# Three fillers in the second and third burst, and fixed steps for the lots between bursts

## The chip, the cores and the metric

One Trainium2 chip, one of its cores. The metric is the device time of one execution of the kernel in microseconds; lower is better.

## The reference

```python
def sm(a, b):                                  # softmax of scaled scores
    s = (a @ b.transpose(0, 2, 1)) / np.sqrt(128)
    e = np.exp(s - s.max(-1, keepdims=True))
    return e / (e.sum(-1, keepdims=True) + 1e-09)
agent_v = sm(agents, k) @ v                    # 4 batches, 49 agents, 12480 keys, width 128
x = (sm(q, agents) @ agent_v).reshape(49920, 128)
h = x @ w_in                                   # 128 x 2048
out = (h * np.cos(h)) @ w_out                  # 2048 x 128
```

All arrays are fp32 (the two weight arrays are float64 on input). Each batch first needs a softmax of 49 agents over its 12480 keys and the product with the values; then each token needs a softmax over 49 agents and a feed-forward layer with h * cos(h).

## The kernel before, in words

Tokens are worked in groups of 960; a batch has 13 groups, the four batches 52. After a start-up of some 65 us, which deals with the keys and values of the first batch, one loop runs over 832 **steps**, 16 for a group. A step does three things: `first_product(n)` (L853, two TensorE matmuls into one of three `ph` tiles in PSUM, then a Sin on ScalarE into `c`, L856), `cubic_part` (L862, one VectorE instruction that makes `r` from `c` and `ph`, and by that frees the `ph` tile), and `second_product(n - 4)` (L878, two matmuls that add into a small PSUM tile `one`; every eighth step ScalarE copies the sum out, L880).

All other work is slipped into these steps by a hand-written plan. Its pieces, called **lots** here, are for the batch that comes next or for groups that come later:

- a **query** (`query_parts`, L510): 16 short matmuls into a small tile `one` (L152), a copy of it to `e` (L527; by VectorE in a burst, by ScalarE elsewhere), the row maximum (L531, VectorE), a subtraction on GpSimd (L533);
- a **values** lot (`add_values`, L585): an addition to `es` on GpSimd (L286), 16 matmuls into a small tile `one` (L301), and their sum taken by VectorE (L307 the first time, L309 later);
- **scores** of the next batch's keys (13 for a batch), and for each group `query_weights` and `query_turned` (L591, L600 to L608), whose steps are the same in both kernels.

Only two small tiles `one` exist (`ps_1`, bufs=2), and one of them is held by the running sum of `second_product`. So one is left for the lots: each must wait until VectorE or ScalarE has emptied the tile of the lot before it.

Exp and Sin are in different ScalarE tables. The Exps are therefore gathered in **bursts**: at step 109, 133 and 157 of each block of 208 steps (`BURSTS`, a block makes one next batch, so there are three blocks with such bursts) ScalarE loads the table of Exp, does one Exp for four or five queries (L575, `query_exp`) and one for four or five groups of keys (L279, `pinned_exp`), and loads the table of Sin again. During that no Sin runs, so no `r` is made and no `ph` tile comes free; `fill(at, todo)` puts up to three lots into this stretch. The first goes into step `at`, the second into step `at + 1` between the sums of the first two queries (L578, VectorE, which wait for the Exp) and the sums of the rest, the third is split over steps `at + 2` and `at + 3`. In the six steps from a burst the order of TensorE, VectorE and ScalarE is held as written.

What `fill` does not take goes into later steps by `extra(n, ...)`, which takes the first free step from n on at certain places of the period of eight (three of eight, or five of eight with `dense=True`).

Of the kernel before, what the change touches and what calls it, by code (L numbers as in the profile page):

```python
# [42 lines left out]
def agent_attention_cos_ffn(ctx, tc, qT, kT, v, v0, v0_rest, agT, w_in, w_out, outT):  # L43
# [432 lines left out]
    with ExitStack() as pools:  # L476
# [145 lines left out]
        BURSTS = (109, 133, 157)  # L622
# [80 lines left out]
        def extra(n, f, *args, dense=False):  # L703


            while n in taken or (n - LAG) % NP not in ((1, 2, 3, 4, 5) if dense else (1, 3, 5)):
                n += 1
            taken.add(n)
            plan(n, f, *args)
            return n  # L710
# [5 lines left out]
        def spread_out(todo, t, end):  # L716

            for i, lot in enumerate(todo):
                t = extra(t, *lot) + 1
                if i + 1 < len(todo):  # L720
                    t += max(0, (end - t) // (len(todo) - i - 1) - 1)
            return t
# [14 lines left out]
        def burst(t, piece, keys=None):  # L737
            assert t + 4 < piece[0] * STEP - 10
            windows.add(t)
            plan(t, query_exp, piece)  # L740
            if keys:
                plan(t, pinned_exp, *keys)
            sums.extend((n, t) for n in piece)
            plan(t + 5, query_inverse, piece)

        def scored(piece, *how):
            return [(query, n, piece, *how) for n in piece]

        def fill(at, todo):

            taken.update(range(at, at + 3))
            parts = [in_parts(*todo.pop(0)) for _ in range(min(3, len(todo)))]
            if parts:
                plan(at, list, parts[0])
            early_plan(at + 1, summed, at, 2)
            if len(parts) > 1:
                early_plan(at + 1, list, parts[1])
            early_plan(at + 1, summed, at, 9)
            for x, n in zip(parts[2:], range(at + 2, at + 9)):
                early_plan(n, next, x)  # L760
                (early_plan if n + 1 < at + 5 else plan)(n + 1, list, x)

        t = spread_out(scored(early), 0, 0) + 2
# [5 lines left out]
        for b in range(1, NB):  # L769
            o, ps = (b - 1) * PER, pieces[b - 1]  # L770

            def valued(k):
                return [(add_values, ab[b], g) for g in range(lots[k][0], sum(lots[k]))]

            qs, ks = scored(ps[0])[ahead:], [(ab[b].scores, g) for g in range(3 if b == 1 else 0, NG)]
            both = []
            while qs or ks:
                both += ks[:3] + qs[:1]
                ks, qs = ks[3:], qs[1:]
            t = spread_out(both, t, o + BURSTS[0] - 14)  # L780
            plan(t, ab[b].top)
            t = extra(t, ab[b].across)
            t = extra(t + 1, ab[b].spread)
            assert t < o + BURSTS[0], (t, o)
            for g, n in lots:
                plan(t, ab[b].shift, g, n, nc.gpsimd)
            nxt = scored(pieces[b][0], False, True)[:2]
            ahead = len(nxt)
            fresh = [scored(ps[1], False, True), scored(ps[2], False, True), nxt]
            for k, at in enumerate(BURSTS):  # L790
                at += o
                burst(at, ps[k], (ab[b], *lots[k]))
                vs, qs = valued(k - 1) if k else [], fresh[k]
                todo = []
                for x in ("qqqqqqq", "vq", "vq")[k]:
                    z = vs if x == "v" else qs
                    if z:
                        todo.append(z.pop(0))
                fill(at, todo)
                t = at + 6  # L800
                if k == 2:
                    vs += valued(2)
                qs, todo = todo, []
                qs += [x for x in fresh[k] if x not in qs]
                qs = [x[:3] if x[0] is query else x for x in qs]
                while vs or qs:
                    todo += qs[:1] + vs[:1]
                    vs, qs = vs[1:], qs[1:]
                if k == 0:
                    todo += [x[:3] for x in fresh[1][:2]]  # L810
                    del fresh[1][:2]
                end = o + BURSTS[min(k + 1, 2)] - 4
                for i, x in enumerate(todo):
                    t = extra(t, *x, dense=k == 2) + (2 if k == 2 else 1)
                    assert k == 2 or x[0] is not query or t < o + BURSTS[k + 1], (t, o, k)
                    if k < 2 and i + 1 < len(todo):
                        t += max(0, (end - t) // (len(todo) - i - 1) - 1)
            plan(t, ab[b].total)
            t = extra(t, ab[b].folded) + 1
            t = extra(t, ab[b].inverse) + 1  # L820
            i = b % 2
            for c in range(DFF // 512):
                t = extra(t, ab[b].project, c, a[i], dense=True) + 1
            t = extra(t, ab[b].project_out, wio, b1[i], b2[i], dense=True)
            plan(t, ab[b].judge)
            t += 1
            assert t < o + PER + 2, (t, o + PER)
        at = (NB - 1) * PER + BURSTS[0]
        t = spread_out([x for piece in pieces[NB - 1] for x in scored(piece)][ahead:], t, at - 6)
# [231 lines left out]
```

## Time and profile before

| | |
|---|---|
| median of 3 runs | 1180.17 us (1177.71 to 1183.73) |
| the profiled execution: its own time | 1180.92 us |
| its span, first to last instruction | 1179.1 us |
| TensorE, VectorE, ScalarE, GpSimd busy | 95%, 90%, 83%, 30% |
| mean granted TensorE clock | 0.977 |

Busy shares are averages over stages with different limits, and a TensorE that runs at half its clock counts as busy. Granted clock 1.00 is 2.4 GHz; the other level is half of it.

### The profile page before, as it was taken

How to read it: one execution, taken by the hardware profiler on the slowest of the kernel's cores; microseconds unless marked ns; L12 is line 12 of the kernel's file. 1: busy time of each engine (PE TensorE's matmuls, PEld its weight loads, DVE VectorE, ACT ScalarE, POOL GpSimd, SP SyncE). 2: the span in 40 equal slices, each digit the busy share in tenths (PEclk: the TensorE clock that was granted, in tenths of full speed). 3: DMA queues.
4: the chain of work that ended last, by engine and by line, in shares of the span. 5: the costliest groups of instructions: out<-in, count | busy, mean ns of one | idle time of the engine just before them, and what ended most of it. 6: DMA issues, size and time to landing. Idle time of an engine off the chain costs nothing.

```text
span 1179.1 us, 17151 instructions
## 1 busy us (share of the span) xinstructions
PE 1122.9 (95%) x6239; PEld 901.8 (76%) x6239; DVE 1061.0 (90%) x1205; ACT 980.1 (83%) x1234; POOL 349.9 (30%) x389
## 2 busy tenths in 40 slices
PE   6899999999999999999899999998999999989996
PEld 3677888787778888787777888877777777767774
DVE  5779999997899999998789999998878999999996
ACT  4778888898678888888778888898777899998995
POOL 1032131752313131463323122264331223122320
PEclk9999999998999999999899999999989999999998
DMA  9733324523201223263220322354240000000001
GB/s 362 288 93 108 101 84 135 167 85 106 96 34 54 91 74 95 81 181 114 85 84 17 101 67 84 106 152 130 68 118 34 34 34 18 34 17 34 18 34 37
DMA packets 37520, 107.74 MB, mean 91 GB/s; under 512 B 4162, under 2 KB 4770, under 8 KB 37426
## 3 DMA queue, kind: packets, MB, share of 16 engines
q1 hardware_dynamic: 37426, 106.55, 28.0%
q8 instruction: 52, 0.85, 0.3%
q14 instruction: 42, 0.34, 0.1%
HBM read 80.97 MB, written 25.56 MB: 90 GB/s over the span
## 4 chain that ended last, share of the span: by engine, by line
PE 70%; DVE 15%; ACT 9%; issue 4%; DMA 1%; SPq 0%; POOL 0%; ACTq 0%; DVEq 0%
PE ph L853 26%; PE one L878 22%; DVE r L862 12%; PE one L152 10%; ACT c L856 5%; PE one L301 3%; PE one L874 2%; PE one L600 2%; PE one L875 1%; DMA c<-qT 1%; PE ph L451 1%; PE one L346 1%; ACT osb L880 1%; ACT L575 1%; ACT s L279 1%
## 5 line engine op out<-in xcount | busy, mean ns | idle before, releaser
L862 DVE SCALAR_TENSOR_TENSOR r<-c,ph 128x960 fp32r<-128x960 f32 x832 | 916.1, 1148 | 60.3 <-ACT c L856 49.7
L856 ACT ACTIVATE c<-ph 128x960 f32<-128x960 f32 x832 | 785.3, 980 | 110.9 <-PE ph L853 99.3
L853 PE MATMUL ph<-pT,a 113*128 113x480 f32 x1664 | 540.2, 404 | 19.7 <-DVE r L862 18.4
L878 PE MATMUL one<-r,w 128*128 128x480 f32 x1664 | 505.4, 392 | 2.1 <-ACT osb L880 1.7
L853 PEld LDWEIGHTS ph<-pT,a 113*128 113x128 f32 x1664 | 293.8, 191 | 134.9 <-DVE r L862 73.6
L878 PEld LDWEIGHTS one<-r,w 128*128 128x128 f32 x1664 | 312.3, 192 | 54.9 <-issue 4.8
L152 PEld LDWEIGHTS one<-ag,xt 128*120 128x120 f32 x1408 | 164.3, 188 | 14.1 <-DVE sums L307 4.2
L152 PE MATMUL one<-ag,xt 128*120 128x49 f32 x1408 | 160.9, 268 | 5.5 <-DVE sums L307 3.0
L591 POOL TENSOR_TENSOR p<-e,rz 120x392 f32<-120x392 f32 x51 | 42.9, 846 | 323.7 <-PE one L600 252.2
L608 POOL TENSOR_TENSOR pT<-p,pT 49x480 fp32r<-49x480 f32 x102 | 124.2, 1217 | 7.8
L533 POOL TENSOR_TENSOR e<-e,mx 120x392 f32<-120x392 f32 x49 | 41.4, 844 | 225.9 <-DVE mx L531 225.6
L607 POOL CAST pT<-p 49x480 fp32r<-49x480 f32 x102 | 59.4, 583 | 114.7 <-ACT p L604 110.1
L880 ACT COPY osb<-one 128x480 f32<-128x480 f32 x104 | 57.9, 557 | 4.1 <-PE one L878 4.1
L301 PE MATMUL one<-vt,s 120*49 120x128 f32 (+1 forms) x624 | 44.9, 289 | 5.2 <-DVE sums L309 5.2
L301 PEld LDWEIGHTS one<-vt,s 120*49 120x49 f32 (+1 forms) x624 | 35.1, 136 | 17.9 <-issue 8.1
L286 POOL TENSOR_TENSOR es<-es,s 120x392 f32<-120x392 f32 x36 | 36.8, 1023 | 37.2 <-ACT s L279 35.5
L275 POOL TENSOR_TENSOR s<-s,mxb 120x1568 f32<-120x1568 f32 (+1 forms) x9 | 31.5, 3534 | 34.1 <-DVE mxb L271 34.1
L875 PE MATMUL one<-pT,b 113*128 113x480 f32 x104 | 39.9, 384 | 0.0
L874 PE MATMUL one<-pT,b 113*128 113x480 f32 x104 | 39.9, 384 | 0.0
L248 ACT COPY s<-one 120x392 f32<-120x392 f32 x36 | 17.5, 487 | 20.8 <-PE one L152 20.8
L527 ACT COPY e<-one 120x392 f32<-120x392 f32 x34 | 16.6, 487 | 20.3 <-PE one L152 20.3
L600 PEld LDWEIGHTS one<-ident,p 120*113 120x113 f32 x204 | 28.6, 179 | 4.6 <-ACT a L347 0.9
(143 smaller groups left out, 542.7 us busy)
## 6 DMA issues: line engine op xcount, KB each, us to landing
outT<-osb SPq DMA_DIRECT2D x51, 480.0 KB, 2.6
xt<-qT SPq DMA_DIRECT2D x49, 480.0 KB, 3.6
xt<-kT SPq DMA_DIRECT2D x39, 480.0 KB, 3.5
vt<-v SPq DMA_DIRECT2D x78, 240.0 KB, 3.9
xt<-kT SPq DMA_DIRECT2D x7, 512.0 KB, 7.7
vt<-v SPq DMA_DIRECT2D x6, 512.0 KB, 5.2
c<-kT SPq DMA_DIRECT2D x5, 512.0 KB, 6.9
vt<-w_in SPq DMA_DIRECT2D x8, 256.0 KB, 7.2
```

The costliest lines, as they stand in the source:

```text
L152: mm = nc.tensor.matmul(ps[:, t, :], xt[:, t * TT:(t + 1) * TT], ag[:, b, :], start=True, stop=True)
L301: mm = nc.tensor.matmul(po[h * HI:h * HI + width], e[:, x * NA:x * NA + width], vt[:, x, :], start=(t == 0), stop=(t == HT - 1))
L600: mm = nc.tensor.transpose(pt[:KR, t * TT:(t + 1) * TT], p_in[n % 2][:, t, :KR], ident[:TT, :TT])
L607: nc.gpsimd.tensor_copy(pT[own, c], p[own])
L608: nc.gpsimd.tensor_sub(pT[other, c], p[own], pT[own, c].bitcast(F32))
L853: nc.tensor.matmul(ph[:, j, :CH], ai[:, f], pTs[q % 3][:, c], start=True, stop=True)
L856: nc.scalar.activation(cos, h, AF.Sin, bias=HALF_PI, scale=1.0)
L862: nc.vector.scalar_tensor_tensor(r, cos, 1.0, h, op0=ALU.subtract, op1=ALU.mult)
L874: nc.tensor.matmul(po, b1[k], pTs[q % 3][:, c], start=False, stop=False)
L875: nc.tensor.matmul(po, b2[k], pTs[q % 3][:, c], start=False, stop=False)
L878: nc.tensor.matmul(po, w1[:, f, :], r[:, j, :], start=(f == 0), stop=(f == NF - 1))
L880: nc.scalar.copy(osb[:, c * CH:(c + 1) * CH], po)
```

## The change

The kinds of the lots that `fill` gets are changed from up to seven queries, "values, query", "values, query" for the three bursts of a block to "query, query, query" and twice "query, values, query". (In the first burst there are three queries either way, as `fill` takes at most three.) The lots after the first burst get steps 117, 125 and 129 of the block, those after the second 141, 145, 149 and 151, in place of an even spread; the lots after the third follow each other as before.

By the rules of `extra` and `fill` the steps of the lots come out so (steps within a block; "b" is in the burst):

| stretch | before | after |
|---|---|---|
| first burst | query b109, b110, b111 | the same |
| up to the second | query 117, 125, 129 | the same |
| second burst | values b133, query b134 | query b133, values b134, query b135 |
| up to the third | query 141, values 143, query 149, values 151 | query 141, values 145, 149, 151 |
| third burst | values 157 (ahead of the Exps), values b157, query b158 | query b157, values b158, query b159 |
| after it | query 165, values 167, 173, 175, 177, 181, 183, 189, 191 | values 165, 167, 173, 175, 177, 181, 183, 189 |
| end of the block | folded 193, inverse 197, project 198, 199, 200, 205, project_out 206 | 191, 193, 197, 198, 199, 200, 205 |

```diff
@@ -792,7 +792,7 @@
                 burst(at, ps[k], (ab[b], *lots[k]))
                 vs, qs = valued(k - 1) if k else [], fresh[k]
                 todo = []
-                for x in ("qqqqqqq", "vq", "vq")[k]:
+                for x in ("qqq", "qvq", "qvq")[k]:
                     z = vs if x == "v" else qs
                     if z:
                         todo.append(z.pop(0))
@@ -809,12 +809,12 @@
                 if k == 0:
                     todo += [x[:3] for x in fresh[1][:2]]
                     del fresh[1][:2]
-                end = o + BURSTS[min(k + 1, 2)] - 4
+                steps = (((117, 125, 129), (141, 145, 149, 151))[k] if k < 2 else ())
                 for i, x in enumerate(todo):
-                    t = extra(t, *x, dense=k == 2) + (2 if k == 2 else 1)
-                    assert k == 2 or x[0] is not query or t < o + BURSTS[k + 1], (t, o, k)
-                    if k < 2 and i + 1 < len(todo):
-                        t += max(0, (end - t) // (len(todo) - i - 1) - 1)
+                    if i < len(steps):
+                        assert t <= o + steps[i], (t, steps)
+                        t = o + steps[i]
+                    t = extra(t, *x, dense=True) + (2 if k == 2 else 1)
             plan(t, ab[b].total)
             t = extra(t, ab[b].folded) + 1
             t = extra(t, ab[b].inverse) + 1
```

## Rows read from the trace of the kernel before

**Rows 1.** The page: engines' busy time, and the granted clock in forty slices.

```profile
PE 1122.9 (95%) x6239; PEld 901.8 (76%) x6239; DVE 1061.0 (90%) x1205; ACT 980.1 (83%) x1234; POOL 349.9 (30%) x389
...
PEclk9999999998999999999899999999989999999998
```

**Rows 2.** Windows (start:end, length, busy by engine, PEclk), cut at starts of Sins.

```profile
214.03:228.74 14.71, 13.81 (x83) 11.32 (x84) 13.53 (x19) 13.51 (x14) 14.26 (x12) 1.00 0.76 209
...
249.63:263.71 14.08, 12.59 (x70) 10.26 (x70) 12.05 (x16) 13.63 (x15) 7.63 (x9) 0.88 0.35 106
263.71:285.69 21.98, 21.51 (x137) 17.87 (x136) 19.88 (x23) 17.34 (x22) 5.66 (x8) 1.00 0.30 90
285.69:304.36 18.67, 16.52 (x83) 13.69 (x84) 12.75 (x20) 14.17 (x14) 7.86 (x8) 0.73 0.27 80
304.36:339.53 35.17, 34.85 (x245) 28.18 (x245) 31.29 (x35) 26.50 (x33) 9.61 (x11) 1.00 0.26 85
...
568.22:586.71 18.49, 15.05 (x83) 12.13 (x84) 13.02 (x20) 14.08 (x14) 7.85 (x8) 0.82 0.28 80
...
814.69:830.36 15.67, 12.62 (x70) 10.26 (x70) 12.18 (x16) 13.72 (x15) 8.68 (x10) 0.89 0.30 94
...
1093.99:1111.57 17.58, 17.17 (x73) 12.41 (x73) 17.24 (x17) 16.18 (x20) 4.46 (x6) 1.00 0.08 29
...
1120.15:1148.44 28.29, 27.72 (x119) 20.25 (x118) 27.63 (x27) 26.28 (x32) 7.21 (x8) 1.00 0.09 36
```

**Rows 3.** Groups of ScalarE instructions in the first block's third burst.

```profile
L856 ACT ACTIVATE c<-ph 128x960 f32<-128x960 f32 x8 | 7.7, 984 | 4.5 <-PE ph L853 4.4
L575 ACT ACTIVATE e<-e 120x1960 f32<-120x1960 f32 x1 | 1.8, 1837 | 0.0
```

**Rows 4.** Timeline of TensorE, first block's third burst (start, us, engine line [idle before]).

```profile
286.42 1.09 PE L301 MATMUL one<-vt,s 120*64 120x128 f32 x16
289.22 1.97 PE L301 MATMUL one<-vt,s 120*64 120x128 f32 x16 [1.72 <-DVE sums L309]
...
292.89 3.28 PE L152 MATMUL one<-ag,xt 128*120 128x49 f32 x16
```

**Rows 5.** Timeline of TensorE, first block's first burst.

```profile
217.84 1.88 PE L152 MATMUL one<-ag,xt 128*120 128x49 f32 x16 [0.47 <-DVE e L527]
219.54 0.69 PE L878 MATMUL one<-r,w 128*128 128x480 f32 x2
220.07 0.60 PE L853 MATMUL ph<-pT,a 113*128 113x480 f32 x2
220.50 1.78 PE L152 MATMUL one<-ag,xt 128*120 128x49 f32 x16
```

**Rows 6.** Timeline of TensorE, first block's second burst.

```profile
249.98 1.09 PE L301 MATMUL one<-vt,s 120*64 120x128 f32 x16
...
253.14 2.26 PE L152 MATMUL one<-ag,xt 128*120 128x49 f32 x16 [1.00 <-DVE sums L307]
```

**Rows 7.** Groups of instructions, whole run (count, busy us, mean ns).

```profile
L531 DVE TENSOR_REDUCE mx<-e 120x8 f32<-120x392 f32 x49 | 27.2, 556 | 2.1 <-ACT e L527 0.4
...
L309 DVE TENSOR_TENSOR sums<-sums,one 113x128 f32<-113x128 f32 x36 | 10.1, 281 | 6.1 <-PE one L301 6.1
...
L527 DVE COPY e<-one 120x392 f32<-120x392 f32 x15 | 8.4, 562 | 9.8 <-PE one L152 9.7
```

**Rows 8.** Timeline of VectorE and ScalarE, the same first burst.

```profile
217.23 0.56 DVE L527 COPY e<-one 120x392 f32<-120x392 f32 x1
217.24 1.51 ACT L575 ACTIVATE e<-e 120x1568 f32<-120x1568 f32 x1
...
218.78 1.03 DVE L578 TENSOR_REDUCE rz<-e 120x8 f32<-120x392 f32 x2 [0.33 <-ACT e L575]
...
219.76 0.57 DVE L527 COPY e<-one 120x392 f32<-120x392 f32 x1
```

**Rows 9.** Transfers issued: queue, count, KB each, median us to landing.

```profile
xt<-qT SPq DMA_DIRECT2D x49, 480.0 KB, 3.6
```

## The prediction

> **What bounds the kernel now.** I read the page first: TensorE is busy for 95% of the span, VectorE for 90%, ScalarE for 83%, and the granted clock dips at a few places only [rows 1]. Shares that near to each other name no bound, so I read it by stage. I cut the steps at the starts of Sins: eight steps of a burst, the 16 or 26 steps behind it, and the same stretches in the fourth block, which has no lots but `query_turned` [rows 2]. In the first block the three bursts take 14.71, 14.08 and 18.67 us for the same eight steps. The reader is to see in those rows which engine fills the stretch. In the second burst ScalarE is busy for 13.63 of 14.08 us: two table loads, two Exps, eight Sins and two copies leave 0.45 us, so nothing that TensorE does there can shorten it much. In the third burst ScalarE is busy for 14.17 of 18.67 us and VectorE for 12.75; the clock is 0.73, so TensorE ran at its lower level for over half of the stretch. That burst is the one with slack: 4.5 us of each.
>
> What ended ScalarE's idle time there is `ph` [rows 3]: 4.4 of 4.5 us wait for `first_product`. TensorE's timeline says why [rows 4]. Two values lots stand one behind the other. The second waits 1.72 us for the small tile, until VectorE has got through the `cubic_part`s queued ahead of the sum; after that gap the clock halves, and the query behind it takes 3.28 us where a query at full clock takes 1.78 [rows 5]. Its VectorE copy, the sums and all later `r` are late by as much, and so is `ph`. The second burst has the same in small: a gap of 1.00 us behind a values lot [rows 6], clock 0.88. In the first burst, where a query comes first, the gap is 0.47 us [rows 5] and the clock stays at 1.00 [rows 2]. The other blocks repeat this: the second burst takes 14.09 us in the second block (the row of the first stands for it) and 15.67 in the third; the third takes 18.49 in the second (clock 0.82) and 18.67 in the third, as in the first.
>
> **The change part by part.** No instruction is added or removed. In each of three blocks two queries move from the steps between bursts into the bursts, and one values lot moves out of the third burst.
>
> *Lots between bursts.* The 16 steps behind the second burst hold two queries and two values lots and take 21.98 us; the same steps with neither take 17.58 in the fourth block: 4.40 us for four lots. The 26 steps behind the third hold one query and eight values lots: 35.17 against 28.29, 6.88 us for nine [rows 2]. If all four cost the same, a query is 1.10 and a values lot 1.10; if both stretches are solved together, a query is 1.52 and a values lot 0.67. I take 1.3 and 0.9. After the change two queries are gone and one values lot has come: -2 x 1.3 + 0.9 = -1.7 us a block, -5.1 in all; the ends are -3.3 (1.10 and 1.10) and -7.1 (1.52 and 0.67). Fixed steps themselves move one lot by two steps (143 to 145) and the block's end by one or two; I cost that at nothing, because the number of lots in the stretch is the same and the deadline of the next block's weights is its own first steps.
>
> *Third burst.* It gets query, values, query in place of values, values, query. VectorE has one copy (0.56) and one maximum (0.56) more and one sum (0.28) less [rows 7]: 12.75 + 0.84 = 13.6 us, still under ScalarE's 14.17. So ScalarE is the floor. What comes on top is the overhang of a burst: 14.71 - 13.53 = 1.2 us in the first burst, whose order of lots the new one resembles, 0.45 in the second [rows 2]. I take 1.0, nearer to the first: 15.2 us. The three third bursts go from 55.83 (18.67 + 18.49 + 18.67) to 45.6: -10.2. The lower end is 14.6 each (-11.9); the upper takes the overhang of the worst second burst, 15.67 - 13.72 = 1.95: 16.1 each (-7.5).
>
> *Second burst.* One query more: VectorE 12.05 + 1.12 = 13.2 us, ScalarE 13.63 as before (a burst's query is copied by VectorE). 13.63 + 1.0 = 14.6 each; three of them 43.8 against 43.84 now: 0. Ends: 14.08 each (-1.6) and 15.6 (+2.9).
>
> *The new wait.* The middle lot is now a values lot, and the third lot must wait for its sum. VectorE does that sum behind the sums of two queries, which wait for the Exp. In the first burst's times [rows 5, 8]: the middle lot starts at 217.84, would end 1.09 us later [rows 6], then come `second_product` and `first_product`, so TensorE is at the third lot at about 219.8. VectorE ends the two sums at 219.81 and the values' sum at 220.1: a gap of about 0.3 us, and some 0.6 in the third burst, whose Exp takes 1.84 [rows 3] in place of 1.51 [rows 8]. Behind the waiting lot on TensorE stand `second_product` and the next `first_product`; their Sins can't run before the table of Sin is back, so ScalarE hides a wait of this size. The gap ahead of the middle lot becomes that of the first burst, about 0.5 us; I bound it by 0.9 in the second burst, whose VectorE ends its `cubic_part`s later.
>
> *A rule that speaks against it.* The gap ends whenever VectorE empties the one free small tile, and that was so in all three bursts [rows 4, 5, 6]; but its size went with the lots' order, from 1.72 to 0.47 us. The Trainium skill, page "Perfetto Trace Analysis", section "Optimization Strategy", holds that the same gap coming back for a stretch can mean that there is too little SBUF or PSUM for the next tile. By that the change, which adds no tile, would leave the gaps, and the time would be that of the second rival below. The sum goes by the rows.
>
> *Transfers.* The moved queries need their 480 KB earlier; one lands in 3.6 us [rows 9]. Three buffers rotate: the query at step 135 takes the buffer that the one at 125 leaves, ten steps earlier, at 1.1 us or more each (17.58 / 16). The first six values lots of a block have six buffers that were left in the block before. So I cost transfers at nothing; without that cover a query would wait up to 3.6 us.
>
> Sum against the profiled execution's 1180.92 us (0.06% above the median of the runs): -10.2 + 0 - 5.1 = -15.3, so 1165.6. With the low ends together 1180.92 - 11.9 - 1.6 - 7.1 = 1160.3, with the high ones 1180.92 - 7.5 + 2.9 - 3.3 = 1173.
>
> **Rivals.** *All of the lost clock comes back.* The share of clock lost in second and third bursts is 0.27 x 18.67 twice, 0.18 x 18.49, 0.12 x 14.08 twice and 0.11 x 15.67 [rows 2]: 18.5 us. If TensorE were what sets the time in all of it, the kernel would take 1180.92 - 18.5 - 5.1 = 1157. Against it: ScalarE's busy time leaves 0.45 us in two of the second bursts, 1.95 in the other and 4.5 in a third. The Trainium skill, "TensorE: Matmul & The Clock Gate", section "Terms", prices a throttled stretch in this way, its length times the share of clock withheld. 7%.
>
> *The bursts still lose the clock.* Two gaps, 0.5 to 0.9 and 0.3 to 0.6 us, now stand close together, and a single one of 1.00 was enough in second bursts [rows 6]. If each burst drops for a short while, as the third block's second burst (15.67 against 14.08, 1.6 us more), third bursts take 16.8 (-5.4), second bursts 16.2 (+4.8), and with the moved lots (-3.3 to -5.1) it comes to 1175 to 1177, within 0.5% of now. 13%.
>
> *Slower: the third lot waits as long as the second values lot does now.* If VectorE has `cubic_part`s or sums queued so that the gap ahead of the third lot reaches 1.7 us, both bursts go as the third does today, and the third lot itself runs at half clock (3.28 for 1.78, +1.5). Third bursts 20.2 (+4.7), second ones 20.2 less the 0.6 us of their shorter Exps, 19.6 (+15.0), lots -5.1: 1195.5. It decides from a gap of about 1.7 us; I work out 0.3 to 0.6. 6%, with a little for whatever else is slower.
>
> **How the numbers follow.** 74% for the forecast; its own range is 1160 to 1173. The predicted time is its sum, 1165.6. The range of 1158 to 1176 adds half of the rival that still loses the clock and leaves out the rest. 0.5% of the time (5.9 us) is about what a measurement of this kernel can tell from no change; below 1174.3 is faster. Faster 0.80 (the forecast and the first rival, less a little of its upper end), same 0.14, slower 0.06.
>
> **What would show it.** In the profile after: third bursts of 15 to 16 us and a clock near 1.00 where 0.73 stood; second bursts about as long as now; 16 steps behind the second burst shorter by 0.4 to 1 us, 26 steps behind the third by 1.1 to 1.5; ScalarE's wait for `ph` in the third burst below 1 us; the gap ahead of the middle lot about 0.5 us and ahead of the third about 0.3 to 0.6. I am wrong if the clock dips stay, if second bursts grow by over 1 us, or if the steps behind the bursts take back what the bursts give.

## The result, and the profile after

The changed kernel takes 1165.14 us (median of 5 runs, 1164.99 to 1169.49), the kernel before beside it 1177.76 us: a ratio of 0.9881, 95% interval 0.9855 to 0.9906. The prediction was 1165.6 us, range 1158 to 1176. The profiled spans are 1179.1 and 1163.3 us, 15.8 us apart.

The windows of the changed kernel, cut at the same Sins as [rows 2]: second burst, 16 steps behind it, third burst, 26 steps behind that, the last 18 steps of the block (all of the first block), and the second burst of the third block:

```profile
250.48:265.43 14.95, 12.91 (x85) 10.20 (x85) 12.72 (x18) 13.79 (x15) 7.85 (x10) 1.00 0.54 161
265.43:286.78 21.35, 21.27 (x138) 17.06 (x136) 19.88 (x24) 16.58 (x21) 5.53 (x7) 1.00 0.29 93
286.78:302.06 15.28, 13.62 (x84) 10.45 (x84) 13.11 (x19) 14.19 (x14) 8.78 (x9) 1.00 0.14 45
302.06:336.48 34.42, 34.42 (x245) 27.16 (x245) 31.35 (x37) 25.99 (x31) 8.78 (x10) 1.00 0.30 96
336.48:359.91 23.43, 22.93 (x99) 16.61 (x97) 22.30 (x30) 20.90 (x26) 7.00 (x10) 1.00 0.05 21
806.38:821.32 14.94, 12.91 (x85) 10.19 (x85) 12.71 (x18) 13.78 (x15) 7.84 (x10) 1.00 0.51 159
```

The one of these stretches of before that [rows 2] does not hold is the end of the block, from the windows of the kernel before:

```profile
339.53:363.42 23.89, 23.66 (x112) 16.86 (x111) 22.08 (x29) 20.37 (x26) 6.33 (x9) 1.00 0.06 22
```

The reader is to see three things in these rows. The third burst fell from 18.67 to 15.28 us with the same eight Sins, and ScalarE's busy time in it did not move (14.17 and 14.19). Its granted clock is 1.00 in place of 0.73; all six changed bursts stand at 1.00. The second burst grew from 14.08 to 14.95 us, at a clock that rose from 0.88 to 1.00. And the steps between are shorter: over three blocks, third bursts went from 55.83 to 45.86 (-10.0), second bursts from 43.84 to 44.83 (+1.0), the 16 steps by -1.9, the 26 steps by -2.4, the ends of the blocks by -1.4; together -14.6 (added before rounding) of the span's 15.8. The other 1.2 us lie in steps whose lots are the same in both kernels, which differ by up to 0.9 us either way: the last block's burst took 15.04 and 14.17, and the first block's first burst began at 214.03 and 214.95.

TensorE's timeline in the first block's third burst after the change, to be read beside [rows 4]:

```profile
287.39 1.78 PE L152 MATMUL one<-ag,xt 128*120 128x49 f32 x16
...
290.59 1.09 PE L301 MATMUL one<-vt,s 120*64 120x128 f32 x16 [0.47 <-DVE e L527]
...
293.12 1.88 PE L152 MATMUL one<-ag,xt 128*120 128x49 f32 x16 [0.38 <-DVE sums L309]
...
297.07 0.70 PE L853 MATMUL ph<-pT,a 113*128 113x480 f32 x2 [0.69 <-DVE r L862]
```

The gap of 1.72 us is gone; three smaller ones stand in its place, and the query's matmuls take 1.88 us where they took 3.28. ScalarE's Sins in that burst wait 0.5 us for `ph` in place of the 4.4 of [rows 3]:

```profile
L856 ACT ACTIVATE c<-ph 128x960 f32<-128x960 f32 x8 | 7.5, 984 | 0.6 <-PE ph L853 0.5
```

The second burst after the change, from the timeline of all engines:

```profile
254.26 1.09 PE L301 MATMUL one<-vt,s 120*64 120x128 f32 x16 [0.78 <-DVE e L527]
...
256.15 0.28 DVE L307 COPY sums<-one 113x128 f32<-113x128 f32 x1
...
258.89 2.22 DVE L862 SCALAR_TENSOR_TENSOR r<-c,ph 128x960 fp32r<-128x960 f32 x2 [1.52 <-ACT c L856]
...
261.03 0.56 DVE L527 COPY e<-one 120x392 f32<-120x392 f32 x1
261.64 0.67 PE L600 MATMUL one<-ident,p 120*113 120x120 f32 x4 [0.84 <-DVE e L527]
```

Here the gap ahead of the middle lot is 0.78 us, there is none ahead of the third (its query at 256.48 has no wait in the timeline), and the third lot's tile is emptied late: its copy at 261.03 stands behind two `cubic_part`s, for the first of which VectorE sat idle for 1.52 us. The matmuls of `query_turned`, which need the tile, wait 0.84 us for it.

### The profile page after: what moved, and what is told of

The parts are those of the page before. It is cut to its first block, busy times and chain, and to the rows that moved or that the text cites. A ratio compares the mean times of both kernels' runs of the same rounds, so it can differ in the third digit from the quotient of the medians.

```text
span 1163.3 us, 17163 instructions
## 1 busy us (share of the span) xinstructions
PE 1110.6 (95%) x6239; PEld 885.4 (76%) x6239; DVE 1063.5 (91%) x1211; ACT 978.4 (84%) x1228; POOL 350.2 (30%) x389
## 4 chain that ended last, share of the span: by engine, by line
PE 65%; DVE 17%; ACT 11%; issue 5%; DMA 1%; SPq 0%; POOL 0%; ACTq 0%; DVEq 0%
PE ph L853 25%; PE one L878 20%; DVE r L862 14%; PE one L152 8%; ACT c L856 6%; PE one L301 3%; PE one L875 1%; PE one L874 1%; PE one L600 1%; DMA c<-qT 1%; ACT L575 1%; PE ph L451 1%; ACT osb L880 1%; ACT s L279 1%; PE one L346 1%
## 5 line engine op out<-in xcount | busy, mean ns | idle before, releaser
L878 PE MATMUL one<-r,w 128*128 128x480 f32 x1664 | 499.9, 388 | 1.4 <-ACT osb L880 1.1
L853 PEld LDWEIGHTS ph<-pT,a 113*128 113x128 f32 x1664 | 288.8, 189 | 135.5 <-DVE r L862 82.7
L878 PEld LDWEIGHTS one<-r,w 128*128 128x128 f32 x1664 | 307.8, 189 | 50.6 <-issue 4.3
L152 PEld LDWEIGHTS one<-ag,xt 128*120 128x120 f32 x1408 | 160.2, 185 | 13.5 <-DVE e L527 3.0
L152 PE MATMUL one<-ag,xt 128*120 128x49 f32 x1408 | 157.9, 265 | 3.8 <-DVE e L527 1.8
L608 POOL TENSOR_TENSOR pT<-p,pT 49x480 fp32r<-49x480 f32 x102 | 124.0, 1216 | 7.8
L607 POOL CAST pT<-p 49x480 fp32r<-49x480 f32 x102 | 59.4, 583 | 114.7 <-ACT p L604 109.8
L880 ACT COPY osb<-one 128x480 f32<-128x480 f32 x104 | 57.9, 557 | 4.8 <-PE one L878 4.8
L301 PEld LDWEIGHTS one<-vt,s 120*49 120x49 f32 (+1 forms) x624 | 33.0, 130 | 17.2 <-issue 9.0
L301 PE MATMUL one<-vt,s 120*49 120x128 f32 (+1 forms) x624 | 42.4, 278 | 3.8 <-DVE e L527 3.8
L275 POOL TENSOR_TENSOR s<-s,mxb 120x1568 f32<-120x1568 f32 (+1 forms) x9 | 31.5, 3530 | 34.2 <-DVE mxb L271 34.2
L600 PE MATMUL one<-ident,p 120*113 120x120 f32 x204 | 29.9, 268 | 2.5 <-DVE e L527 2.5
```

Of the source, the lines that this page charges most:

```text
L152: mm = nc.tensor.matmul(ps[:, t, :], xt[:, t * TT:(t + 1) * TT], ag[:, b, :], start=True, stop=True)
L301: mm = nc.tensor.matmul(po[h * HI:h * HI + width], e[:, x * NA:x * NA + width], vt[:, x, :], start=(t == 0), stop=(t == HT - 1))
L600: mm = nc.tensor.transpose(pt[:KR, t * TT:(t + 1) * TT], p_in[n % 2][:, t, :KR], ident[:TT, :TT])
L607: nc.gpsimd.tensor_copy(pT[own, c], p[own])
L608: nc.gpsimd.tensor_sub(pT[other, c], p[own], pT[own, c].bitcast(F32))
L853: nc.tensor.matmul(ph[:, j, :CH], ai[:, f], pTs[q % 3][:, c], start=True, stop=True)
```

## Experiments

The theory: a gap on TensorE lets its clock fall, and at the low clock `ph` comes late for ScalarE; that was most of the third burst's excess. Rivals: the clock only follows, and VectorE's queue and the place of the lots make the burst long; or what gains is the third lot under the Exps. A **dip** is here a stretch in which the granted clock is at its lower level, and the **later place** is the `first_product` behind the Exps that waits for the first `cubic_part` to free a `ph` tile. Where no interval is given, a kernel was measured in one execution. Spans are those of the profiled runs (before 1179.1, changed 1163.3). The diffs are against the changed kernel unless told otherwise.

**More work in the gap.** The kernel before, with two values lots of a block (the first of the second burst and the one at step 157) multiplied twice.

```diff
-            for t in range(HT):
+            for again in range(2 if g in (0, 3) and ordered[0] else 1):
+                for t in range(HT):
...
```

> The kernel before, with the 16 matmuls of the first values lot of the second burst and of the values lot at step 157 done twice into the same tile (the second time starts the sum anew, so the output is the same). TensorE gets about 1.1 us more work just ahead of the gap. Theory (the gap lets the clock fall, and the low clock makes the third burst long): the gap in the third burst shrinks from 1.72 to about 0.7 us and the one in the second from 1.00 to about 0, the clock stays at 1.00, third bursts take 15.5 to 16.5 us in place of 18.6, second ones 14.1 to 14.5; the span is 6 to 9 us shorter although work was added. Rival (VectorE's queue and the place of the lots make the burst long, the clock only follows): third bursts stay at 18.6 or grow by up to 1 us, the span is 0 to 3 us longer.

It measured 1172.07 us (median of 8 runs; ratio to before 0.9934, interval 0.9911 to 0.9957), span 1170.2. The third bursts and, last but one, a second burst in its windows:

```profile
286.21:301.72 15.51, 12.96 (x99) 10.72 (x100) 12.85 (x20) 13.98 (x14) 7.87 (x8) 1.00 0.34 96
565.70:581.22 15.52, 12.95 (x99) 10.71 (x100) 12.86 (x20) 13.98 (x14) 7.87 (x8) 1.00 0.34 97
809.06:824.74 15.68, 13.51 (x86) 11.13 (x86) 12.11 (x16) 13.75 (x15) 8.58 (x10) 0.89 0.29 95
846.71:862.22 15.51, 12.95 (x99) 10.71 (x100) 12.86 (x20) 13.97 (x14) 7.87 (x8) 1.00 0.44 128
```

And TensorE's timeline in the first third burst (this kernel's lines stand one lower, L302 for L301):

```profile
286.93 1.96 PE L302 MATMUL one<-vt,s 120*64 120x128 f32 x32
289.74 1.09 PE L302 MATMUL one<-vt,s 120*64 120x128 f32 x16 [0.85 <-DVE sums L310]
...
297.40 0.67 PE L854 MATMUL ph<-pT,a 113*128 113x480 f32 x2 [1.61 <-DVE r L863]
```

Work was added, no lot was moved, and the kernel became 0.66% faster. The gap is 0.85 us, the clock stays at 1.00, and each third burst is 3.0 to 3.2 us shorter, 9.3 us for the three. The second values lot starts 3.5 us into the burst in both kernels, so the wait for VectorE ahead of it ends as late as before, and the clock is what differs. This is the theory's case and rules out the first rival. In the second burst the gap behind the values lot went, but one of 2.07 us stood at the later place; the bursts took 14.11, 14.09 and 15.67, as before. A burst with two lots has a second place at which TensorE runs dry.

Where in a burst the dip falls decides what it costs. The kernel before in its first and its third second burst, each cut ahead of the dip and in it:

```profile
249.63:254.40 4.77, 3.77 (x34) 2.80 (x34) 3.33 (x5) 4.74 (x6) 0.00 (x0) 1.00 0.65 200
254.50:257.85 3.35, 3.35 (x12) 2.93 (x12) 2.94 (x6) 3.32 (x3) 1.98 (x2) 0.50 0.44 119
...
814.69:824.45 9.76, 6.71 (x49) 5.12 (x48) 7.64 (x12) 9.70 (x10) 3.52 (x4) 1.00 0.49 151
824.55:827.85 3.30, 3.30 (x11) 2.86 (x12) 2.98 (x3) 1.66 (x3) 2.70 (x5) 0.50 0.00 0
```

In the first the dip lies under the second Exp and the load of the Sin table: ScalarE is busy for 3.32 of its 3.35 us, and the burst of 14.08 us is as long as those of 14.09 and 14.11 that have no dip. In the second it comes at the later place: ScalarE is busy for 1.66 of 3.30 us, and the burst takes 15.67.

**The order alone.** Query before values in the burst; the values lot at step 157 stays.

```diff
-                for x in ("qqq", "qvq", "qvq")[k]:
+                for x in ("qqq", "qv", "qv")[k]:
-                steps = (((117, 125, 129), (141, 145, 149, 151))[k] if k < 2 else ())
+                steps = (((117, 125, 129), (141, 143, 149, 151, 157))[k] if k < 2 else ())
```

> Two lots in the second and third burst as before, but the query first and the values second; every other lot at its step of before, the values lot at step 157 ahead of the third burst too. Theory: second bursts lose their gap of 1.00 us and the dip, 14.1 to 14.3 us; in the third burst the query now waits for the sum of the values lot at 157, the gap of about 1.7 us and the low clock stay, 17.5 to 19 us; the span is within 3 us of before. Rival (query first is what counts in itself): third bursts fall to 15 to 16 us, the span by some 9 us.

Span 1178.3. Third bursts 17.8, 17.8 and 17.8; TensorE's timeline in the first shows the gap where the theory puts it, and the query behind it at half clock:

```profile
290.10 3.43 PE L152 MATMUL one<-ag,xt 128*120 128x49 f32 x16 [1.73 <-DVE sums L309]
```

The second bursts did not all get the 14.1 us I expected: 14.10, 15.68 and 15.68, all three with a gap of 2.45 to 2.47 us at the later place, and the last two with a dip there. The rival (query first is what counts) is out: the third bursts did not fall to 15 or 16 us.

**The lot at step 157 alone.** Values, query in the bursts, but no lot within six steps ahead of the third.

```diff
-                for x in ("qqq", "qvq", "qvq")[k]:
+                for x in ("qqq", "vq", "vq")[k]:
-                steps = (((117, 125, 129), (141, 145, 149, 151))[k] if k < 2 else ())
+                steps = (((117, 125, 129), (141, 143, 145, 149, 151))[k] if k < 2 else ())
```

> Bursts as before (values, query), but the values lot at step 157 goes to step 145, so that no lot stands within six steps ahead of the third burst. Theory: the third burst becomes like the second of before, a gap of about 1.0 us and at most a short dip, 14.7 to 16.5 us; the three values lots between cost about 0.9 us each; the span is 5 to 8 us shorter. Rival (the third lot under the Exps is what gains): third bursts stay above 17.5 us, the span is within 2 us of before.

Span 1175.5: 3.6 us gained where I expected 5 to 8, as two of the three third bursts, 17.08, 14.71 and 17.09 us, lie above the 14.7 to 16.5 that I gave. Its windows show those of the first and the second block, with the same instructions in the same order:

```profile
288.00:305.08 17.08, 13.71 (x67) 10.96 (x67) 13.14 (x19) 14.10 (x14) 7.82 (x8) 0.80 0.20 59
571.60:586.31 14.71, 11.33 (x68) 8.90 (x68) 12.57 (x19) 13.97 (x14) 7.86 (x8) 1.00 0.21 67
```

TensorE's timeline at the later place in each of them:

```profile
298.40 1.14 PE L853 MATMUL ph<-pT,a 113*128 113x480 f32 x2 [2.71 <-DVE r L862]
...
582.00 0.66 PE L853 MATMUL ph<-pT,a 113*128 113x480 f32 x2 [2.73 <-DVE r L862]
```

The gap ahead of the second lot is 0.66 us in both; the later one is 2.7 us in both. In the first block the granted clock is 0.50 from 297.5 us, still in the gap, to 304.3; in the second it stays at 1.00. That is a clean price: 14.71 us at full clock, 17.08 with the dip. The 18.67 us of before were 14.7 and some 4 us of low clock and of the lot at 157 with its gap, and the third lot's part is to fill the later gap (0.69 us in the changed kernel).

**Values first, three lots.**

```diff
-                for x in ("qqq", "qvq", "qvq")[k]:
+                for x in ("qqq", "vqq", "vqq")[k]:
```

> The changed kernel with the burst's three lots in the order values, query, query; all else as changed. Theory: the gap behind the values lot comes back (about 1.0 us in both bursts), dips come back in some of the six bursts, second bursts take 15 to 16 us and third ones 15.3 to 16.5; the span is 2 to 6 us longer than the changed kernel's 1163.3. Rival (three lots in the burst and no lot ahead of it are enough, whichever comes first): bursts within 0.3 us of the changed kernel's 14.94 and 15.28, span within 1 us.

Span 1165.6. Third bursts 15.29 each, second ones 18.04, 14.94 and 14.95. The first two second bursts in its windows:

```profile
249.38:267.42 18.04, 17.05 (x85) 14.67 (x85) 13.03 (x18) 13.76 (x15) 8.09 (x10) 0.72 0.45 134
530.02:544.96 14.94, 13.05 (x85) 10.20 (x85) 12.71 (x18) 13.78 (x15) 7.73 (x10) 1.00 0.53 158
```

Both have a gap of 0.98 to 0.99 us behind the values lot; after one the clock fell for some 10 us, after the other it held. Without a dip the order of the three lots changes nothing, so within a burst the rival is right on the time of five of the six, and the theory has one dip in six for it, where I had expected dips in several. One dip is too few to say that this order is the riskier one.

**One burst at a time.** First the third alone, then the second alone.

```diff
-                for x in ("qqq", "qvq", "qvq")[k]:
+                for x in ("qqq", "vq", "qvq")[k]:      # third alone; lots at 141, 143, 145, 149, 151
+                for x in ("qqq", "qvq", "vq")[k]:      # second alone; lots at 141, 145, 149, 157
```

> Only the third burst gets query, values, query; the second keeps values, query, and the lots between them stand at 141, 143, 145, 149, 151. Theory (the third burst's clock is most of the gain): third bursts 15.3 us, second ones 14.1 or 15.7 as before, 16 steps behind the second burst about 22.9, 26 behind the third about 34.4; span about 1167 to 1170. Rival (the gain is shared by both bursts): span above 1171.

> Only the second burst gets query, values, query; the third keeps values, query with the values lot at step 157 ahead of it. Theory: second bursts 14.9 us, steps behind them about 1 us shorter, third bursts still 17.5 to 18.7 with the low clock; span within 3 us of 1179. Rival: span below 1173.

Changed third burst: span 1175.0, third bursts 15.31, 15.29, 15.29 and second ones 15.67, 15.66, 15.66. That is above the expected 1167 to 1170 and on the rival's side of 1171. But 3.2 us of it are second bursts, in the order of before, that took 15.7 us in all three blocks in place of one, and 4.6 us are a dip in a burst that the edit does not touch, the first burst of the first block, 19.30 us where every other kernel of the same order there but one took 14.7. Without these two it would be some 1167 us. The windows of that first burst, of the part of it up to the dip, of the dip, and of the third burst:

```profile
214.31:233.61 19.30, 19.22 (x83) 17.10 (x84) 14.22 (x20) 13.53 (x14) 15.81 (x13) 0.65 0.55 153
214.31:216.75 2.44, 2.36 (x19) 2.30 (x20) 2.44 (x4) 2.42 (x4) 2.44 (x2) 1.00 0.00 0
216.80:230.40 13.60, 13.60 (x51) 11.96 (x51) 9.33 (x14) 8.46 (x8) 13.15 (x12) 0.50 0.66 186
...
292.64:307.95 15.31, 13.66 (x84) 10.46 (x84) 13.13 (x19) 14.21 (x14) 8.78 (x9) 1.00 0.15 45
```

Changed second burst: span 1172.5, second bursts 14.94, 14.94, 14.95; the 16 steps 20.36 for 21.98; and the third bursts:

```profile
285.16:303.62 18.46, 14.92 (x83) 12.00 (x84) 12.83 (x19) 14.05 (x14) 7.42 (x8) 0.82 0.28 81
566.87:582.35 15.48, 11.95 (x83) 9.71 (x84) 12.67 (x19) 13.94 (x14) 7.44 (x8) 1.00 0.30 96
845.48:864.12 18.64, 16.48 (x83) 13.65 (x84) 12.56 (x19) 14.16 (x15) 7.39 (x8) 0.73 0.36 106
```

All three are in the order of before, with a gap of 1.92 us; the second kept its clock. That is the price of the dip in the order of before: 3.2 us (18.64 and 15.48). I had put this span within 3 us of before; it gained 6.6, and so came out on the rival's side (below 1173). Of that, 3.0 are the burst of 15.48 and 4.8 the query gone from the 16 steps, less 1.0 for the longer second bursts.

**The third lot's tile freed earlier.** The third lot wholly ahead of the `cubic_part` that waits for the first Sin, in all bursts.

```diff
-            for x, n in zip(parts[2:], range(at + 2, at + 9)):
-                early_plan(n, next, x)
-                (early_plan if n + 1 < at + 5 else plan)(n + 1, list, x)
+            for x in parts[2:]:
+                early_plan(at + 2, list, x)
...
-                if late and n - 1 in cosines:
+                if late and n - 1 in cosines and n - 2 not in windows:
                     cubic_part(n - 1)
                 early_plan.run(n)
+                if late and n - 1 in cosines:
+                    cubic_part(n - 1)
```

> The changed kernel, with the whole third lot of each burst ahead of the cubic part that waits for the first Sin after the Exps, so that VectorE copies the third query out of the small tile while it would sit idle (1.5 us), and the gap of 0.84 us ahead of the turning matmuls goes. Theory (the second burst's 0.86 us over the burst with two lots is that late copy): second bursts 14.1 to 14.5 us, third ones 14.8 to 15.2, first ones 14.3 to 14.7; span 1160 to 1162. Rival (the copy and the maximum then stand ahead of the first cubic parts and make them late): bursts 0 to 0.6 us longer, span 1163 to 1167.

It measured 1168.74 us (6 runs; ratio to before 0.9914, interval 0.9888 to 0.9941). That interval overlaps the changed kernel's, but the profile shows why it is no better: the span is 1167.8. Second bursts 14.68 and third ones 15.02 are each 0.26 us shorter, which the late copy explains in part; but first bursts went from 14.7 to 18.69, 17.30 and 15.94. The timeline of the first block's first burst:

```profile
226.81 0.56 DVE L531 TENSOR_REDUCE mx<-e 120x8 f32<-120x392 f32 x1 [2.25 <-POOL e L533]
...
228.48 0.69 PE L852 MATMUL ph<-pT,a 113*128 113x480 f32 x2 [2.73 <-DVE r L861]
```

The third query's maximum waits 2.25 us for one of two `mx` tiles, which GpSimd holds until it has subtracted; GpSimd is behind because it shifts the keys at that time (L275, one instruction of 4.03 us up to 222.1, with L607 and L608 behind it up to 225.9). With the query ahead of the `cubic_part`s, that wait holds up `ph`, and TensorE with it.

**Values last.** Query, query, values in both bursts; one run, then several beside the changed kernel on one chip.

```diff
-                for x in ("qqq", "qvq", "qvq")[k]:
+                for x in ("qqq", "qqv", "qqv")[k]:
```

> The changed kernel with the lots in the order query, query, values. Theory: the third lot leaves its tile by one sum of 0.28 us in place of a copy and a maximum of 1.1 us, the middle lot by a copy; second bursts 14.4 to 14.9 us, third ones 14.9 to 15.3; span 1160.5 to 1163.5, no dips. Rival (the values lot in the middle is what keeps the gaps short): dips come back, bursts over 15.5 us, span over 1165.

> The changed kernel once more, as the measure for the three beside it: 1163 to 1167 us, six changed bursts of 14.9 and 15.3 us. If the place of a burst in time decides whether the clock falls, an execution that starts otherwise may show a dip of 3.4 us or more and be 1 to 4 us longer.

> Query, query, values in both bursts, timed: 1160 to 1163 us, 0.2 to 0.5% below the changed kernel. Theory: the second burst's 14.3 and the third's 14.96 us hold (the third lot's tile is free after one sum of 0.28 us), any dip costs 0.8 to 2.5 us more. Rival (the one look was a lucky placement): 1164 us or more.

The first run's span was 1159.3. The several runs: the changed kernel 1165.44 us (4 runs, 1164.57 to 1169.21; ratio to before 0.9883, interval 0.9858 to 0.9908), values last 1160.94 (5 runs, 1160.05 to 1163.17; ratio 0.9839, interval 0.9820 to 0.9857), 0.4% less. In the first run's windows, a second burst, the 16 steps behind it, a third burst, and a second burst with a dip:

```profile
250.18:264.44 14.26, 13.00 (x87) 10.69 (x87) 13.02 (x18) 13.64 (x15) 8.65 (x10) 1.00 0.54 166
264.44:285.13 20.69, 20.69 (x136) 16.67 (x134) 19.14 (x23) 16.46 (x21) 4.69 (x7) 1.00 0.29 96
285.13:300.09 14.96, 13.22 (x84) 10.59 (x84) 13.65 (x21) 13.97 (x14) 8.71 (x9) 1.00 0.12 34
802.26:817.35 15.09, 14.31 (x87) 11.88 (x87) 13.36 (x18) 13.64 (x15) 8.85 (x10) 0.89 0.51 154
```

Compared with the changed kernel, a second burst gains 0.7, the 16 steps 0.7 and a third burst 0.3 us. Dips did come back, in three of the six second bursts of the two profiles, at 0.8 us each.

The runs of the changed kernel say one thing more. Of its nine, here and in the result, seven took 1164.6 to 1165.7 us at a mean granted clock of 0.993 to 0.995, and two took 1169.2 and 1169.5 at 0.987. Those two lost clock that the two profiles do not show; where is not known.

**Two steps further.** All three queries in the second burst, with values lots at 141, 143, 149, 151; and values last, with its sum ahead of the `cubic_part`, in second and third bursts only.

```diff
-                for x in ("qqq", "qvq", "qvq")[k]:
+                for x in ("qqq", "qqq", "qqv")[k]:     # three queries
+                for x in ("qqq", "qqv", "qqv")[k]:     # sum early, with the edits below
...
+                if at % PER in BURSTS[1:]:
+                    early_plan(at + 2, list, x)
+                    continue
...
-                if late and n - 1 in cosines:
+                if late and n - 1 in cosines and not (n - 2 in windows and (n - 2) % PER in BURSTS[1:]):
                     cubic_part(n - 1)
                 early_plan.run(n)
+                if late and n - 1 in cosines:
+                    cubic_part(n - 1)
```

> The second burst takes all three queries of the third piece and its four values lots follow at 141, 143, 149, 151; the third burst query, query, values. Theory: second bursts 14.9 to 15.3 us (a late copy again), the 16 steps behind them 20.2 to 20.5, so even with the kernel with values last; span 1158 to 1162. Rival (a query under the Exps is always worth more than it costs there): second bursts at 14.4, span below 1157.

> Query, query, values, with the third lot's sum ahead of the cubic part that waits for the first Sin, in second and third bursts only. Theory (what is left over ScalarE's busy time is the late release of the small tile): second bursts 14.0 to 14.2 us, third ones 14.5 to 14.8, span 1156.5 to 1159. Rival (the gap moves on to the first product that waits for the first cubic part, as in the kernel with the third query early): no gain, span 1159 to 1163, or dips and more.

Three queries: span 1160.6, second bursts 14.93 to 14.95, 16 steps 21.0, third bursts 14.96 to 14.98: no better than values last, and the 16 steps cost 0.5 us more than I expected. The sum early: 1161.42 us (4 runs; ratio 0.9840, interval 0.9820 to 0.9859), level with values last. Its bursts are the shortest of all, 14.03 and 14.77 in the first block, but the 16 steps are 0.1 us longer than values last's, and its profiled run had a dip in the untouched first burst, 19.36 us. Its three other runs have mean clocks of 0.989 and 0.990, where this profile without that dip would have 0.993 (an estimate from its 13.7 us at half clock). So each of them seems to have lost clock as well, which would hide what the shorter bursts gain; where, no profile shows.

## Why the prediction was right

**What bounds.** The slack was in the third burst and the clock made most of it: shown by the kernel with more work, and by the bursts of one order with a dip and without (18.64 and 15.48 us, 17.08 and 14.71). ScalarE's busy time was the floor there as the prediction has it: 14.19 of 15.28 us.

**Third burst.** Predicted 15.2, measured 15.28; -10.2 against -10.0. The overhang over ScalarE came to 1.1 us, where I took 1.0. Of this term the experiments gave the parts: the clock gave back 3.2 us (18.67 to 15.5, in the kernel with more work and in the burst of 15.48), the lot at 157 with its gap 0.8 (15.48 to 14.71), and the third lot costs 0.6 (14.71 to 15.28).

**Second burst.** Predicted 14.6, measured 14.94, a sum of +1.0 in place of 0. This term was mis-sized. The overhang over ScalarE's 13.79 is 1.15 us for the 1.0 that I took, and ScalarE itself was busy 0.16 us longer. (In the kernel before it makes three copies there, L880 twice and L604; the prediction counts two, but its 13.63 us are right.) What I left out of the working is the third lot's exit: its copy stands behind two `cubic_part`s and holds the tile until 261.6. Against the bursts with two lots and no dip (14.09 to 14.11) the third lot costs 0.84 us; with the values lot last it costs 0.2 (14.26), and with its sum early as well nothing (14.03), so the late exit is what cost. What the third lot buys is steadiness. Of the 15 second bursts with two lots in five profiles (before, more work, order alone, lot at 157 alone, third burst alone) eight took 15.66 to 15.68, each with a dip at the later place, which makes the mean of the 15 14.9; the nine with query, values, query all took 14.94 to 14.96. The prediction read the gap of 1.00 us as the cause of the second bursts' lost clock and took 1.6 us for a short dip from the burst of 15.67; the dip behind that gap cost nothing (14.08), and the 1.6 us belong to the later place, which the prediction does not name.

**Lots between bursts.** Predicted -1.7 us a block, measured -0.62 (16 steps), -0.79 (26 steps) and -0.46 (end of the block), -1.87. The sum is near, but the prediction miscounted the lots of two stretches. The window of the 26 steps held one query and seven values lots, not eight; the last values lot began behind its end, 339.53, on TensorE's timeline of before:

```profile
340.95 1.09 PE L301 MATMUL one<-vt,s 120*64 120x128 f32 x16
```

So in the 26 steps a values lot took the place of the query, and the values lot that is gone is missing at the end of the block; I had 1.1 to 1.5 us for the 26 steps and nothing for the end. In the 16 steps the experiments give the prices: a query 1.6 us (21.98 to 20.36 with one less) and a values lot 0.9 (21.98 to 22.88 with one more), for the 1.3 and 0.9 that I took.

**The new wait.** Predicted about 0.3 us ahead of the third lot in the second burst and 0.6 in the third; there was none and 0.38. Ahead of the middle lot 0.78 and 0.47, near the 0.5 to 0.9 given. No dip followed in any of the 18 bursts with query, values, query in four profiles (the changed kernel twice, third burst alone, second burst alone).

**The total.** That it came within 0.5 us is in part luck. The second bursts' +1.0 was made up for by 0.5 us more from the lots between bursts and by 1.2 us in steps that the change does not touch; and the sum starts from one run of the kernel before, 1180.92 us, whose runs went from 1177.19 to 1183.73. Between the medians of the result the gain is 12.6 us, where the sum has 15.3.

**The rivals.** All of the lost clock coming back: it did not. The 18.5 us were worked out as clock lost in both kinds of burst; in third bursts alone it is 0.27 x 18.67 twice and 0.18 x 18.49, 13.4 us, and the kernel with more work, whose third bursts lost none, got 9.3 us of it. The rest cost nothing. I take it that TensorE was waiting or ScalarE set the time in those stretches, as in the second burst of 14.08 us; for the third bursts no run shows it apart. The price by the Trainium skill ("TensorE: Matmul & The Clock Gate", "Terms"), throttled time times the share withheld, thus came out too high here, 13.4 for 9.3 us. The rival with dips left in the bursts did not come (clock 1.00 in all six), nor the one in which the third lot waits for 1.7 us (none, and 0.38). The rule that a gap that comes back may mean too little room for the next tile (the Trainium skill, "Perfetto Trace Analysis", "Optimization Strategy") names what TensorE waits for here, but no tile had to be added: with the same two small tiles the gap went from 1.72 to 0.47 us.

**What stays open.** Why the clock falls after one gap and not after the same gap in the same order elsewhere (17.08 and 14.71 us, 18.64 and 15.48, 18.04 and 14.94). In the first burst of 19.30 us it fell 2.5 us in, with TensorE busy for 2.36 of the 2.44 us up to there, and no gap just ahead of it but the 0.78 us that the bursts of 14.7 have as well (0.80). So a gap is not all that counts, and no run here settled what else does. The six bursts without a dip are what these profiles show, not a guarantee; two of nine runs lost clock somewhere.

## What to carry to other kernels

When an engine that looks busy runs at a lower clock after a gap, price the gap with what follows it: here a gap of 1.7 us brought 3.2 us of low clock into a burst of 18.7. Look in each stretch for the engine whose busy time is the floor; only the part of the low clock that pushes that engine is to be had: a dip under the Exp and the table load cost nothing, one as long behind them 1.6 us. With one tile for the fillers, put none just ahead of a burst and put last the one whose tile is emptied fastest (0.4% here). Test a theory of the clock by adding redundant work in the gap.

## What the runs showed that I had not expected

Work added to the busiest engine made the kernel 0.66% faster, because it kept TensorE at its higher level (third bursts from 18.6 to 15.5 us). And the same instructions in the same order take 14.7 or 17 to 19 us in different blocks or runs: in two of twelve experiments the first burst of the first block, untouched by their edits, took 19.3 us at a clock of 0.65.
